# Attention and a long convolution on one core: VectorE's exponential passes in halves, new planning clocks, half a q projection moved forward

## The chip, the cores and the metric

The kernel runs on one core of a Trainium2 chip. The metric is device time in microseconds of a run. The core's engines are TensorE (PE in the profile; PEld is its weight load), VectorE (DVE), ScalarE (ACT), GpSimd (POOL) and SyncE (SP, which here issues most DMAs). Each takes its instructions in the order in which they were written for it, and they wait for one another by semaphores.

## The reference

Two independent computations over 2048 positions and 512 channels, whose results are put side by side. All inputs are bf16.

```python
# A: attention, 32 heads of 16 channels
q, k, v = split(x @ wqkv)
scores = einsum("bhqd,bhkd->bhqk", q, k) * 16 ** -0.5
a = einsum("bhqk,bhkd->bhqd", softmax(scores), v)  ->  merged heads @ wo

# B: a short shift convolution, then a convolution as long as the sequence
kv = (sum over t of k_pad[:, t:t+2048, :] * shift_k[:, 3-t]) * v
y = irfft(rfft(kv, 4096) * rfft(ssm_k, 4096))[:2048] + kv * ssm_D
b = q * y
out = concatenate([a, b], axis=-1)
```

The scores have 32 x 2048 x 2048 elements, and each of them needs an exponential.

## The kernel before

**Blocks and chunks.** Attention is cut into 2048 blocks of 128 keys by 512 queries of one head. A block of scores is one matmul into one bank of the matmul accumulator PS (line L678 in `emit_qk`), and a chunk `T` is three blocks, at the start and the end two: 695 chunks. Chunks use banks 0 to 2 and 3 to 5 in turn. ScalarE takes the exponential of a chunk in one instruction (L685), from PS into the tile PT. The products with v (`emit_pv`, L773) are matmuls that add up in another bank; a column of ones beside v gives the sums by which the result is divided (`finish_group`, L797 to L814).

**Blocks on VectorE.** For some chunks the third block is left out of ScalarE's instruction, and VectorE makes its exponential. Scores are scaled so that they count in units of 1/65536 of a power of two. A first operation, the fix (L701, in `exp_on_dve`), clamps the block, adds the exponent's offset and writes whole numbers into the tile EI: the upper half of such a number is the exponent, the lower half the fraction. When a set of two or four blocks is full, `passes` records five operations for it (L725, L727, L728, L729 and L731), which work out a polynomial of the fraction in fp16 tiles, and a last one (L735, two blocks at a time) that puts it into the number. Its upper 16 bits, read as bf16, are the exponential, and L773 reads them straight from EI. Each operation waits for the one before it.

**Other work.** TensorE also makes the projections to q, k and v (L395, L402, L436), the short convolution (L460), the long one as matmuls over shifted weights, which are streamed by 512 DMAs into the ring WR (L926), the output projection (L850), and fillers that add zeros (L1071). VectorE copies the results out of PS.

**What sets the order.** The program is planned while it is built. Each engine has a planning clock (`Eng.t`); each recorded operation advances it by a cost in microseconds, and its result counts as seen a little later (`seen_after`). `dve_choice` decides from these clocks whether a chunk gives a block to VectorE: not when VectorE's clock is over `FIX_BEHIND` ahead of TensorE's, not in the last `LAST` chunks, in sets of four from chunk `FULL_AT` on. The passes go into the list `dve_fill`, and are written between VectorE's other operations where they fit ahead of the next fix, as `FIX_LATE` and `NEXT` allow, or when a block falls due. TensorE's queue is filled likewise: `emit_bg` puts projections and convolution between scores and products as far as the clock says that there is time. Ahead of the loop over chunks, the first projection of q and 128 keys are made; the second projection of q is made behind the first chunk's scores, in `bg_step` at `T == 0`.

Of the kernel before, what the change touches and what calls it, by code (L numbers as in the profile page):

```python
# [6 lines left out]
ALU = mybir.AluOpType  # L7
# [28 lines left out]
R_PT = 5  # L36
# [14 lines left out]
OCT = 2.0 ** 16  # L51
ROOT0, ROOT1 = 0.0127173909, 0.9900476185
C0, C1 = 0.3043078141, 0.0780240431
FS = 128.0
BITS = 2.0 ** 23
QSCALE = SCALE * math.log2(math.e) * OCT
FIX_LO = -118.0 * OCT
FIX_ADD = 127.0 * OCT
FULL_AT = 110
UNIT = 1  # L60
OPK = 2
PRODK = 2
TIME = 0.7
FULL = 4
APART = 1
OPEN_STEPS = 4
ROOM = {2: 4.0, 4: 8.0}
LATE = 9.0
CLOSE = 6.0
LAST = 12  # L70
PAIRS_AT_END = 22
SPLIT = 2
FIX_BEHIND = 1.2
NEXT = -0.2
PV_HOLD = 3
LAG_US = 0.068
SPAN = 3.4
SHARE = 0.9
SLACK = 0.06
FIX_LATE = 0.7  # L80
FILL_LATE = 0.5
HARD = 0.7
OPE = 1
FETCH = 256
FETCH_AT = 192
# [25 lines left out]
class Eng:  # L111
# [24 lines left out]
    def op(self, fn, deps=(), inc=True, us=None, late=FILL_LATE, fill=False, counted=False):  # L136
        waits = []
        ready = max([0.0] + [self.at[(id(d[0]), d[1])] for d in deps if d])
        while self.fill and not fill and self.t + self.fill[0][0] <= ready + late:
            self.fill.pop(0)[1]()  # L140
        for d in deps:
            if d is None:
                continue
            sm, v = d
            self.t = max(self.t, self.at[(id(sm), v)])
            if self.seen.get(id(sm), 0) < v:
                self.seen[id(sm)] = v
                waits.append((sm, v))
        if counted:
            c = Count()  # L150
            fn(c)
            n = c.n + max(len(waits) - 1, 0)
            late, self.fetch = self.stall(n, us)
            self.t += late
            self.count += n
        self.t += self.us if us is None else us
        self.last = [x for x in self.last if x[0] > self.t - SPAN] + [(self.t, self.us if us is None else us)]
        if inc:
            self.n += 1
            self.at[(id(self.sem), self.n)] = self.t + self.seen_after  # L160
        self.ops.append((waits, fn, self.sem if inc else None))
        return (self.sem, self.n)
# [21 lines left out]
def bass_concat_heads__mha_block__ssm_conv_h3__prompt_kernel(  # L184
# [24 lines left out]
    def sb(name, shape, dt=BF16):  # L209
# [47 lines left out]

    at = {}
    pe, act, dve, pool, sp = [Eng(sem(n), at, us, after) for n, us, after in (
        ("s_pe", 0.5, 0.11), ("s_act", 0.5, 0.16), ("s_dve", 0.69, 0.06), ("s_pool", 0.5, 0.1), ("s_sp", 0.05, 0.1))]  # L260

    queue = [0.0]

# [150 lines left out]
    def evac_unit(u, bank, h, eng=None):  # L414
        kind = u[0]
        if kind == "q":
            _, qb, g = u
            assert qb != 1 or all((c, 2 + g // 4) in h_prod for c in range(4))
            hh = dve.op(lambda e: e.tensor_scalar(QT[:, qb % 2, g, :], PS[:, bank, :], QSCALE, None, ALU.mult),  # L419
                        [h])  # L420
            h_q[(qb, g)] = hh
        else:
            _, o, sc = u
            dst = KTo[:, o, sc * 512:(sc + 1) * 512]
            if eng is act:
                hh = act.op(lambda e: e.activation(dst, PS[:, bank, :], ACT.Copy), [h])
            else:
                hh = dve.op(lambda e: e.tensor_copy(dst, PS[:, bank, :]), [h])  # L428
            h_k[(o, sc)] = hh
        bank_free[bank] = hh  # L430
# [20 lines left out]
    def unit(u, bank, eng=None):  # L451
        evac_unit(u, bank, pe_unit(u, bank), eng)
# [88 lines left out]
    h = k_part(0, 128)  # L541
    h_k0 = act.op(lambda e: e.activation(KTo[:, 0, 0:128], PS[:, 7, 0:128], ACT.Copy), [h])
    bank_free[7] = h_k0
    evac_unit(("q", 0, 0), 6, hq)


    NBLK = NQB * NG * KT * 4
    size, plan, b_ = [], {}, 0
    while b_ < NBLK:
        T = len(size)  # L550
        n = min(2 if (T % 2 == 1 and T < N_EARLY) or NBLK - b_ <= TAIL else 3, NBLK - b_)
# [106 lines left out]
    h_blk = {}  # L658
    h_ptfree, pt_used = {}, {}
# [9 lines left out]
    def emit_qk(T):  # L669
        bl, banks = chunks[T]  # L670
        deps = qk_deps(T)
        assert None not in deps or T < 8

        def fn(e):
            ins = None
            for b, bank in zip(bl, banks):
                qb, g, kt, s = blk(b)
                ins = e.matmul(PS[:, bank, :],  # L678
                               lhsT=KTo[32 * s:32 * s + 32, g // 2, kt * 128:(kt + 1) * 128],
                               rhs=QT[32 * s:32 * s + 32, qb % 2, g, :],  # L680
                               start=True, stop=True, tile_position=(32 * s, 0))
            return ins
        h = pe.op(fn, deps, us=0.32)
        n = len(bl) - (bl[-1] in on_dve)
        h_exp[T] = act.op(lambda e: e.activation(PT[:, T % R_PT, 0:n * QB],  # L685
                                                 PS[:, banks[0]:banks[0] + n, :].rearrange("p b f -> p (b f)"),
                                                 ACT.Exp, scale=math.log(2.0) / OCT),
                          [h] + h_ptfree.get(T - R_PT, []), us=0.427 * n + 0.047)
        assert T < R_PT or pt_used[T - R_PT] == sum(b not in on_dve for b in chunks[T - R_PT][0])
        for b, bank in zip(bl[:n], banks):  # L690
            bank_free[bank] = h_blk[b] = h_exp[T]
        if n < len(bl):
            bank_free[banks[n]] = exp_on_dve(bl[n], banks[n], h, T)

    h_set = [None]
# [12 lines left out]
    def passes(s):  # L708
        ei = EI[:, s.off:s.off + s.k, :]
        frac = ei.bitcast(UINT16).rearrange("p i (f e) -> p i f e", e=2)[:, :, :, 0]  # L710
        ea, eb = EA[:, 0:s.k, :], EX[:, 0:s.k, :] if s.cap == 4 else EA[:, 2:2 + s.k, :]
        old = [st0["x0"]] if s.cap == 4 and all(o.cap == 2 for o in sets if o is not s) else []
        eg = ea.bitcast(BF16)

        now_g = blk_group(rest[0])
        due = len(chunks) + min((len(rest_of[now_g]) + 2) // 3 if blk_group(x) <= now_g else 22 for x in s.blks) + 1
        st = {"h": None}

        def step(rate, fn, *deps):
            us = 0.155 + 0.533 * s.k / rate  # L720

            def run():
                st["h"] = dve.op(fn, [st["h"] or h_set[0]] + list(deps), us=us, fill=True)
            dve_fill.append((us, run, due))
        step(2, lambda e: e.tensor_scalar(eb, frac, FS / OCT, -FS * ROOT0, ALU.mult, ALU.add),  # L725
             *s.fix, *old)
        step(4, lambda e: e.tensor_scalar(ea, eb, FS * (ROOT0 - ROOT1), None, ALU.add))  # L727
        step(2, lambda e: e.tensor_tensor(ea, ea, eb, ALU.mult))  # L728
        step(4, lambda e: e.tensor_scalar(eb, eb, C1 * BITS / FS ** 3, (C0 + C1 * ROOT0) * BITS / FS ** 2,  # L729
                                                 ALU.mult, ALU.add))  # L730
        step(2, lambda e: e.tensor_tensor(eg, ea, eb, ALU.mult))  # L731

        def last(i0, i1, us):
            def run():
                h_set[0] = dve.op(lambda e: e.scalar_tensor_tensor(ei[:, i0:i1, :], ei[:, i0:i1, :], BITS / OCT, eg[:, i0:i1, :],  # L735
                                                                   ALU.mult, ALU.add), [st["h"], h_set[0]], us=us, fill=True)
                for x in s.blks[i0:i1]:
                    h_blk[x] = h_set[0]
            dve_fill.append((us, run, due))
        for i0 in range(0, s.k, SPLIT):  # L740
            last(i0, min(i0 + SPLIT, s.k), 0.155 + 0.533 * min(SPLIT, s.k - i0))

    dve_fill = dve.fill

# [338 lines left out]
    def bg_step(T, lim):  # L1083
        if T >= 150 and not st["wop"] and len(h_v) == 2 * KT and len(h_k) == 16:
            st["wop"] = True
            load_wop(pe_last())
        for item in list(later):
            if item[0] <= T:
                later.remove(item)
                item[1]()  # L1090
        if T == 0:
            unit(("q", 0, 1), 5)
            h = k_part(128, 512)
            bank_free[7] = h_k[(0, 0)] = dve.op(lambda e: e.tensor_copy(KTo[:, 0, 128:512], PS[:, 7, 128:512]), [h])
            return
        if h_kzall[0]:
            load_wr(T)
            if not h_qn:
                load_qn(0, [h_kzp[15]])
        st["time"] = min(st["time"] + (0.78 if T >= CONV_AT else 0.4 if T >= N_EARLY else 0.45), 1.1)  # L1100
        rest = NB * C // 4 - NB * st["qd"] - st["lag"]
        if T >= N_EARLY:
            st["lags"] = min(st["lags"] + rest / max(CONV_END - T, 1.0), 3.0 * LAGS)
        if run_jobs(T, lim):
            run_conv(T, lim)
# [107 lines left out]
    for T in range(NT + 3):  # L1213
# [7 lines left out]
        for b in [b for batch in pvs for b in batch]:  # L1221
            n = blk_group(b)
# [32 lines left out]
    for t in range(4):  # L1255
        wait_busy(when_of(h_otn[(NQB * NG - 1, 2 * (t // 2) + 2)]), 0)
        h = op_mm(qb, t, 7, 8, banks[t])
# [55 lines left out]
```

## Time and profile before

| | |
|---|---|
| median of three runs | 846.3 us (845.18 to 847.07) |
| the profiled execution, its own time | 846.82 us |
| its span in the trace | 845.0 us |
| busy: PE, DVE, ACT, POOL | 85%, 82%, 98%, 7% |
| granted TensorE clock, mean | 0.997 |

Busy is the time in which an engine has at least one instruction under way, so that overlapping instructions count once, while the mean duration of a group counts each in full. Line numbers such as L685 are lines of the kernel before. A bracket behind a row of the timeline says how long the engine had been idle and what ended that.

### The profile page before, as it was taken

What the parts mean: (1) busy time and instruction counts of PE and PEld (TensorE: products, weight loads), DVE (VectorE), ACT (ScalarE), POOL (GpSimd) and SP (SyncE); (2) the same over time, 40 slices, a digit from 0 to 9 for tenths busy, and PEclk for the clock granted to TensorE, in tenths of its full rate; (3) what the DMA queues carried; (4) which work ended last, traced back from release to release, by engine and by line L of the source; (5) the groups of instructions that cost most, each with busy time, mean ns of one, the idle gap of its engine ahead of it and who ended that gap; (6) DMA issues with size and microseconds to landing.
All of it is one profiled execution on the core that took longest, in us unless ns stands there. A gap on an engine that the chain in (4) does not pass through costs nothing.

```text
span 845.0 us, 30581 instructions
## 1 busy us (share of the span) xinstructions
PE 720.2 (85%) x13944; PEld 311.9 (37%) x13944; DVE 696.8 (82%) x937; ACT 829.2 (98%) x701; POOL 62.8 (7%) x68
## 2 busy tenths in 40 slices
PE   8888889888888889888888888888888888988887
PEld 3332333333333332334344433233444444334422
DVE  4226888879999899898999899889899888888884
ACT  6999999999999999999999999999999999999996
POOL 3893000000000001000000000000000000100000
PEclk9999999999999999999999999999999999999999
DMA  9989302059768662487666869237688899646820
GB/s 247 302 313 250 96 1 74 2 139 254 235 187 262 188 212 73 156 250 222 214 217 221 285 214 279 78 106 268 198 256 266 288 294 312 211 157 219 293 54 26
DMA packets 123970, 167.36 MB, mean 198 GB/s; under 512 B 50496, under 2 KB 55616, under 8 KB 123584
## 3 DMA queue, kind: packets, MB, share of 16 engines
q1 hardware_dynamic: 120864, 162.77, 62.1%
q8 instruction: 110, 1.80, 0.8%
q10 hardware_dynamic: 2400, 1.05, 0.6%
q0 software_dynamic: 576, 1.57, 0.5%
q14 instruction: 20, 0.16, 0.1%
HBM read 143.14 MB, written 16.52 MB: 189 GB/s over the span
## 4 chain that ended last, share of the span: by engine, by line
ACT 94%; PE 3%; DMA 1%; DVE 1%; SPq 0%; issue 0%; ACTq 0%
ACT PT L685 93%; DMA WR<-kz_scratch 1%; PE PS L678 1%; PE PS L526 0%; PE PS L436 0%; PE PS L773 0%; SPq L269 0%; PE PS L850 0%; PE PS L926 0%; DVE VAF L447 0%; PE PS L395 0%; PE PS L402 0%; DVE QT L419 0%; ACT QT L866 0%; PE PS L374 0%
## 5 line engine op out<-in xcount | busy, mean ns | idle before, releaser
L685 ACT ACTIVATE PT<-PS 128x1536 bf16<-128x1536 f32 (+1 forms) x695 | 825.2, 1585 | 3.3 <-PE PS L678 3.1
L678 PE MATMUL PS<-QT,KTo 32*128 32x512 bf16 x2048 | 272.1, 385 | 106.7 <-ACT PT L685 91.5
L773 PE MATMUL PS<-PT,VAF 128*32 128x512 bf16 x1828 | 225.7, 390 | 1.1 <-DVE VAF L447 0.7
L926 PE MATMUL PS<-WR,KV 128*22 128x64 bf16 (+15 forms) x8192 | 180.8, 214 | 3.4 <-DMA WR<-kz_scratch 3.0
L701 DVE TENSOR_SCALAR EI<-PS 128x512 int32<-128x512 f32 x220 | 150.2, 688 | 38.9 <-PE PS L678 38.1
L678 PEld LDWEIGHTS PS<-QT,KTo 32*128 32x128 bf16 x2048 | 67.8, 91 | 270.1 <-ACT PT L685 255.6
L926 PEld LDWEIGHTS PS<-WR,KV 128*22 128x22 bf16 (+15 forms) x8192 | 148.6, 120 | 48.4 <-issue 22.5
L735 DVE SCALAR_TENSOR_TENSOR EI<-EI,EA 128x1024 int32<-128x1024 int32 x110 | 134.1, 1219 | 2.1
L773 PEld LDWEIGHTS PS<-PT,VAF 128*32 128x32 bf16 x1828 | 53.9, 93 | 97.9 <-issue 91.9
L725 DVE TENSOR_SCALAR xT<-EI 128x2048 f16<-128x2048 uint16 x48 | 58.7, 1223 | 1.3
L728 DVE TENSOR_TENSOR EA<-EA,xT 128x2048 f16<-128x2048 f16 x48 | 58.4, 1217 | 0.5
L731 DVE TENSOR_TENSOR EA<-EA,xT 128x2048 bf16<-128x2048 f16 x48 | 58.3, 1215 | 0.5
L269 POOL DMA_DIRECT2D out_dram<-OUTA x12 | 7.9, 660 | 661.4 <-DVE OUTA L857 460.6
L1071 PE MATMUL PS<-IDN,ZR 128*32 128x512 bf16 (+3 forms) x664 | 52.4, 330 | 0.0
L773 PE MATMUL PS<-EI,VAF 128*32 128x512 bf16 x220 | 45.3, 410 | 0.0
L395 PE MATMUL PS<-xT,WQP 128*128 128x512 bf16 x128 | 40.3, 385 | 3.3 <-DVE KTo L428 1.7
L850 PE MATMUL PS<-WKV,OTN 128*128 128x512 bf16 x128 | 37.2, 384 | 1.3 <-DVE OUTA L857 0.7
L727 DVE TENSOR_SCALAR EA<-xT 128x2048 f16<-128x2048 f16 x48 | 33.1, 691 | 1.3
L729 DVE TENSOR_SCALAR xT<-xT 128x2048 f16<-128x2048 f16 x48 | 32.9, 686 | 0.5
L797 DVE STREAM_TRANSPOSE DT<-PS 128x512 f32<-128x512 f32 x30 | 21.4, 713 | 11.4 <-PE PS L773 11.4
L419 DVE TENSOR_SCALAR QT<-PS 128x512 bf16<-128x512 f32 x32 | 21.8, 682 | 8.8 <-PE PS L395 8.8
L447 DVE CAST VAF<-PS 128x512 bf16<-128x512 f32 (+1 forms) x17 | 11.2, 656 | 17.1 <-PE PS L436 17.0
(74 smaller groups left out, 367.1 us busy)
## 6 DMA issues: line engine op xcount, KB each, us to landing
WR<-kz_scratch SPq DMA_DIRECT2D x512, 256.0 KB
kz_scratch<-WR SPq DMA_DIRECT2D x16, 752.0 KB, 5.8
QN<-in_B_q_dram SPq DMA_DIRECT2D x16, 128.0 KB, 4.0
out_dram<-KV SPq DMA_DIRECT2D x16, 128.0 KB, 4.5
out_dram<-OUTA POOLq DMA_DIRECT2D x12, 128.0 KB, 2.2
QT<-in_B_ssm_k_dram SPq DMA_DIRECT2D x1, 1024.0 KB, 5.5
EI<-in_B_ssm_k_dram SPq DMA_DIRECT2D x1, 1024.0 KB, 8.9
OTN<-in_B_v_dram SPq DMA_DIRECT2D x1, 1024.0 KB, 5.9
```

Source lines behind the costliest of these rows:

```text
L395: return e.matmul(PS[:, bank, :], lhsT=WQP[:, dc, g, :], rhs=xT[:, dc, qb * 512:(qb + 1) * 512], start=(dc == 0), stop=(dc == 3))
L678: ins = e.matmul(PS[:, bank, :], lhsT=KTo[32 * s:32 * s + 32, g // 2, kt * 128:(kt + 1) * 128], rhs=QT[32 * s:32 * s + 32, qb % 2, g, :], ...
L685: h_exp[T] = act.op(lambda e: e.activation(PT[:, T % R_PT, 0:n * QB], PS[:, banks[0]:banks[0] + n, :].rearrange("p b f -> p (b f)"), ACT.E ...
L701: s.fix.append(dve.op(lambda e: e.tensor_scalar(EI[:, i, :], PS[:, bank, :], FIX_LO, FIX_ADD, ALU.max, ALU.add), [h] + old + [x for o in s ...
L725: step(2, lambda e: e.tensor_scalar(eb, frac, FS / OCT, -FS * ROOT0, ALU.mult, ALU.add), *s.fix, *old)
L728: step(2, lambda e: e.tensor_tensor(ea, ea, eb, ALU.mult))
L731: step(2, lambda e: e.tensor_tensor(eg, ea, eb, ALU.mult))
L735: h_set[0] = dve.op(lambda e: e.scalar_tensor_tensor(ei[:, i0:i1, :], ei[:, i0:i1, :], BITS / OCT, eg[:, i0:i1, :], ALU.mult, ALU.add), [s ...
L773: ins = e.matmul(PS[32 * s:32 * s + 32, pvb(qb * NG + g), :], lhsT=VAF[:, kt, h * VW:h * VW + 32], rhs=rhs, start=(order[b] == 0), stop=(o ...
L850: ins = e.matmul(PS[:, bank, :], lhsT=OTN[:, oslot(qb * NG + g), t * 128:(t + 1) * 128], rhs=WOP[:, g, :], start=(g == 0), stop=(g == NG - 1))
L926: ins = e.matmul(PS[32 * c:32 * c + NW - 2 * n, BGB, col:col + 64], lhsT=KV[:, 2 * n:NW, 4 * qd + c], rhs=w, start=(n == 0), stop=(n == NB ...
L1071: ins = e.matmul(PS[32 * c:32 * c + 32, pvb(n), 0:128 * k], lhsT=ZR[:, :], rhs=IDN[:, :].rearrange("p (m d) -> p m d", m=1).broadcast_to([ ...
```

## The change

- **Passes in halves.** `passes` now cuts a set into two halves (of two blocks, or of one in a set of two). Each of the six operations is recorded for the first half and then for the second, and each waits for the operation before it on its own half, not for the other half's. The last operation's results count as done by halves.
- **Planning clocks.** VectorE's operations are planned 0.084 us shorter, and their results are seen 0.12 us later instead of 0.06. An exponential of n blocks is planned at 0.41 n + 0.1 instead of 0.427 n + 0.047.
- **Thresholds and weights of the planner**, among them those shown below.
- **Half a q projection.** Two of the four matmuls of the second q projection stand ahead of the loop over chunks, the other two where all four stood.

```diff
-FULL_AT = 110
+FULL_AT = 90
-TIME = 0.7
+TIME = 0.8
-CLOSE = 6.0
-LAST = 12
+CLOSE = 4.0
+LAST = 10
-SPLIT = 2
-FIX_BEHIND = 1.2
-NEXT = -0.2
+DVE_OVER = 0.084
+DVE_SEEN = 0.12
+FIX_BEHIND = 1.6
+NEXT = -0.1
-FIX_LATE = 0.7
+FIX_LATE = 0.4
+Q1 = 2
...
-        self.t += self.us if us is None else us
+        self.t += (self.us if us is None else us) - (DVE_OVER if self.us == 0.69 else 0.0)
...
-        ("s_pe", 0.5, 0.11), ("s_act", 0.5, 0.16), ("s_dve", 0.69, 0.06), ("s_pool", 0.5, 0.1), ("s_sp", 0.05, 0.1))]
+        ("s_pe", 0.5, 0.11), ("s_act", 0.5, 0.16), ("s_dve", 0.69, DVE_SEEN), ("s_pool", 0.5, 0.1), ("s_sp", 0.05, 0.1))]
...
     evac_unit(("q", 0, 0), 6, hq)
+    pe_unit(("q", 0, 1), 5, range(Q1))
...
-                          [h] + h_ptfree.get(T - R_PT, []), us=0.427 * n + 0.047)
+                          [h] + h_ptfree.get(T - R_PT, []), us=0.41 * n + 0.1)
...
-        st = {"h": None}
-
-        def step(rate, fn, *deps):
-            us = 0.155 + 0.533 * s.k / rate
+        st, width = {}, (s.k + 1) // 2
+        def piece(rate, make, deps, i0, i1, ends):
+            us = 0.155 + 0.533 * (i1 - i0) / rate
 
             def run():
-                st["h"] = dve.op(fn, [st["h"] or h_set[0]] + list(deps), us=us, fill=True)
-            dve_fill.append((us, run, due))
+                h = dve.op(make(slice(i0, i1)), [st.get(i0, h_set[0])] + deps, us=us, fill=True)
+                st[i0] = h
+                if ends:
+                    h_set[0] = h
+                    for x in s.blks[i0:i1]:
+                        h_blk[x] = h
+            return us, run, due
+
+        def step(rate, make, deps=(), ends=False):
+            for i0 in range(0, s.k, width):
+                dve_fill.append(piece(rate, make, list(deps), i0, min(i0 + width, s.k), ends))
...
-            unit(("q", 0, 1), 5)
+            evac_unit(("q", 0, 1), 5, pe_unit(("q", 0, 1), 5, range(Q1, 4)))
```

Counted over the whole order, VectorE gets 244 fixes instead of 220; ScalarE's 695 exponentials are 414 of three blocks and 281 of two, instead of 438 and 257; the sets are 52 of four blocks and 18 of two, instead of 48 and 14, and their passes 840 instructions instead of 420; the fillers on TensorE fall from 664 matmuls to 564. The lines of the changed kernel are numbered two to nine higher: the fix is L704, the passes L737 to L744, the exponential L688, the scores L681, the q projection L397.

TensorE, at the start: warm-up, turning x, the first q projection (into PS from WQP), 128 keys, the first chunk's scores. Before:

```order
L395 MATMUL PS<-xT,WQP 128x512 x4
L538 MATMUL PS<-xT,WKV 128x128 x4
L678 MATMUL PS<-QT,KTo 128x512 x3
L395 MATMUL PS<-xT,WQP 128x512 x4
L538 MATMUL PS<-xT,WKV 128x384 x4
L678 MATMUL PS<-QT,KTo 128x512 x2
```

And now:

```order
L397 MATMUL PS<-xT,WQP 128x512 x4
L540 MATMUL PS<-xT,WKV 128x128 x4
L397 MATMUL PS<-xT,WQP 128x512 x2
L681 MATMUL PS<-QT,KTo 128x512 x3
L397 MATMUL PS<-xT,WQP 128x512 x2
L540 MATMUL PS<-xT,WKV 128x384 x4
L681 MATMUL PS<-QT,KTo 128x512 x2
```

Two of the second projection's matmuls moved from behind the first scores to ahead of them.

VectorE, in the middle of the run: the passes of a set of four (EI, EA and xT are the sets' tiles) with fixes (EI from PS) and copies between them. Before:

```order
L731 TENSOR_TENSOR EA<-EA,xT 128x2048
L735 SCALAR_TENSOR_TENSOR EI<-EI,EA 128x1024 x2
L725 TENSOR_SCALAR xT<-EI 128x4x512
L727 TENSOR_SCALAR EA<-xT 128x2048
L728 TENSOR_TENSOR EA<-EA,xT 128x2048
L701 TENSOR_SCALAR EI<-PS 128x512
L729 TENSOR_SCALAR xT<-xT 128x4x512
L701 TENSOR_SCALAR EI<-PS 128x512 x3
```

And now:

```order
L743 TENSOR_TENSOR EA<-EA,xT 128x1024 x2
L744 SCALAR_TENSOR_TENSOR EI<-EI,EA 128x1024 x2
L861 CAST OUTA<-PS 128x512
L737 TENSOR_SCALAR xT<-EI 128x2x512 x2
L739 TENSOR_SCALAR EA<-xT 128x1024 x2
L740 TENSOR_TENSOR EA<-EA,xT 128x1024 x2
L741 TENSOR_SCALAR xT<-xT 128x2x512
L704 TENSOR_SCALAR EI<-PS 128x512
L741 TENSOR_SCALAR xT<-xT 128x2x512
L704 TENSOR_SCALAR EI<-PS 128x512
```

Each pass is now two instructions of half the size, one for each half, and a fix may stand between the two.

ScalarE, in the first third: exponentials of three blocks (1536 columns) and of two (1024), in runs. Before:

```order
L685 ACTIVATE PT<-PS 128x1536 x8
L685 ACTIVATE PT<-PS 128x1024 x4
L685 ACTIVATE PT<-PS 128x1536 x6
L685 ACTIVATE PT<-PS 128x1024 x4
L685 ACTIVATE PT<-PS 128x1536 x8
L685 ACTIVATE PT<-PS 128x1024 x4
```

And now:

```order
L688 ACTIVATE PT<-PS 128x1536 x6
L688 ACTIVATE PT<-PS 128x1024 x4
L688 ACTIVATE PT<-PS 128x1536 x5
L688 ACTIVATE PT<-PS 128x1024 x4
L688 ACTIVATE PT<-PS 128x1536 x6
L688 ACTIVATE PT<-PS 128x1024 x4
```

Each run of four short ones is a set of four on VectorE; fewer long ones stand between two such sets.

More of the change, by code (lines that the diff above doesn't have):

```diff
@@ L725, in passes @@
[L725 to L741, printed above, removed]
+                h = dve.op(make(slice(i0, i1)), [st.get(i0, h_set[0])] + deps, us=us, fill=True)
@@ new lines, in run @@
+                st[i0] = h
[7 more added lines that the diff above has]
+                dve_fill.append(piece(rate, make, list(deps), i0, min(i0 + width, s.k), ends))
+        step(2, lambda sl: lambda e: e.tensor_scalar(eb[:, sl], frac[:, sl], FS / OCT, -FS * ROOT0, ALU.mult, ALU.add),
+             s.fix + old)
@@ new lines, in passes @@
+        step(4, lambda sl: lambda e: e.tensor_scalar(ea[:, sl], eb[:, sl], FS * (ROOT0 - ROOT1), None, ALU.add))
+        step(2, lambda sl: lambda e: e.tensor_tensor(ea[:, sl], ea[:, sl], eb[:, sl], ALU.mult))
+        step(4, lambda sl: lambda e: e.tensor_scalar(eb[:, sl], eb[:, sl], C1 * BITS / FS ** 3,
+                                                     (C0 + C1 * ROOT0) * BITS / FS ** 2, ALU.mult, ALU.add))
+        step(2, lambda sl: lambda e: e.tensor_tensor(eg[:, sl], ea[:, sl], eb[:, sl], ALU.mult))
@@ L743, in bass_concat_heads__mha_block__ssm_conv_h3__prompt_kernel @@
+        step(1, lambda sl: lambda e: e.scalar_tensor_tensor(ei[:, sl], ei[:, sl], BITS / OCT, eg[:, sl], ALU.mult, ALU.add),
+             ends=True)
     dve_fill = dve.fill
```

## The prediction

> **What bounds the kernel now.** I read the page first: busy time of each engine, the chain that ended last, the largest group.
>
> ```profile
> PE 720.2 (85%) x13944; PEld 311.9 (37%) x13944; DVE 696.8 (82%) x937; ACT 829.2 (98%) x701; POOL 62.8 (7%) x68
> ACT PT L685 93%; DMA WR<-kz_scratch 1%; PE PS L678 1%; PE PS L526 0%; PE PS L436 0%; PE PS L773 0%; SPq L269 0%; PE PS L850 0%; PE PS L926 0%; DVE VAF L447 0%; PE PS L395 0%; PE PS L402 0%; DVE QT L419 0%; ACT QT L866 0%; PE PS L374 0%
> L685 ACT ACTIVATE PT<-PS 128x1536 bf16<-128x1536 f32 (+1 forms) x695 | 825.2, 1585 | 3.3 <-PE PS L678 3.1
> ```
>
> ScalarE's exponentials are the kernel: 695 of them fill 825.2 us of a span of 845.0 and are 93% of the chain, with 3.3 us of idle before them in all. Whatever shortens this row shortens the kernel, as long as nothing else begins to hold it up. The mean of 1585 ns is no price, though: 695 times it is 1102 us, so neighbours overlap. The price is the step from one start to the next, read from ScalarE's timeline with a window that is opened further and further:
>
> ```profile
> 400.62 2.72 ACT L685 ACTIVATE PT<-PS 128x1536 bf16<-128x1536 f32 x2
> 400.62 4.06 ACT L685 ACTIVATE PT<-PS 128x1536 bf16<-128x1536 f32 x3
> 400.62 4.98 ACT L685 ACTIVATE PT<-PS 128x1536 bf16<-128x1536 f32 x4
> ```
>
> One more exponential adds 1.34 us or 0.92 us: three blocks of scores, or two. Check: the order has 438 of three and 257 of two before, and 438 x 1.34 + 257 x 0.92 = 823 us, against 825.2 in the row. **A block of scores that VectorE takes is worth 0.42 us of ScalarE.**
>
> The second question is who serves VectorE and who waits for it: the table of waits, then a stretch of the windows without start and end.
>
> ```profile
> DVE EI L701 <- PE PS L678: 38.1, 91, 2.5
> ACT PT L685 <- PE PS L678: 3.1, 5, 1.0
> PE PS L678 <- DVE EI L701: 1.4, 5, 0.4
> 110.00:830.00 720.00, 614.08 (x13102) 273.04 (x13099) 637.92 (x834) 718.40 (x603) 7.92 (x12) 1.00 0.63 196
> ```
>
> VectorE (the third figure with a count, 637.92) is idle 82 us of these 720, and its first operation on a block (L701, the "fix") waited 38.1 us for scores in the whole run: VectorE is early. The scores (L678) waited for a fix five times, 1.4 us in all. So VectorE has room, and TensorE's clock is at 1.00.
>
> **The change part by part.** *More blocks on VectorE.* The order has 244 fixes instead of 220, and exponentials of 414 and 281 instead of 438 and 257. ScalarE loses 24 x 0.42 = **10.1 us**, all of it on the path. That is the main term; the new costs and thresholds of the planner count only through it and through where things stand.
>
> *The passes in halves.* VectorE's timeline shows what a pass costs behind one that it needs, and behind one that it doesn't:
>
> ```profile
> 512.63 1.22 DVE L731 TENSOR_TENSOR EA<-EA,xT 128x2048 bf16<-128x2048 f16 x1
> 513.88 2.49 DVE L735 SCALAR_TENSOR_TENSOR EI<-EI,EA 128x1024 int32<-128x1024 int32 x2
> 516.40 1.23 DVE L725 TENSOR_SCALAR xT<-EI 128x2048 f16<-128x2048 uint16 x1
> 517.66 0.70 DVE L727 TENSOR_SCALAR EA<-xT 128x2048 f16<-128x2048 f16 x1
> 518.39 1.23 DVE L728 TENSOR_TENSOR EA<-EA,xT 128x2048 f16<-128x2048 f16 x1
> 519.53 0.69 DVE L701 TENSOR_SCALAR EI<-PS 128x512 int32<-128x512 f32 x1
> 520.13 0.68 DVE L729 TENSOR_SCALAR xT<-xT 128x2048 f16<-128x2048 f16 x1
> 520.73 1.45 DVE L701 TENSOR_SCALAR EI<-PS 128x512 int32<-128x512 f32 x2
> ```
>
> L725 to L727 is 1.26 us for an operation of 1.23: a dependent pass starts 0.03 to 0.04 after the end. But L728 to the fix is 1.14 for 1.23, the fix to L729 0.60 for 0.69, and L729 to the next fix 0.60 for 0.68: an independent operation starts about 0.085 **before** the end. A chain of whole passes on a set of four blocks therefore costs 1.26 + 0.73 + 1.26 + 0.73 + 1.25 + 2.52 = 7.75 us. Halves taken in turn are independent neighbours, at the durations of these forms:
>
> ```profile
> L701 DVE TENSOR_SCALAR EI<-PS 128x512 int32<-128x512 f32 x220 | 150.2, 688 | 38.9 <-PE PS L678 38.1
> L735 DVE SCALAR_TENSOR_TENSOR EI<-EI,EA 128x1024 int32<-128x1024 int32 x110 | 134.1, 1219 | 2.1
> L939 DVE CAST YB<-PS 128x256 bf16<-128x256 f32 x23 | 9.7, 421 | 6.8 <-PE PS L926 6.0 <-PE PS L1071 0.4 <-PE PS L773 0.4
> L725 DVE TENSOR_SCALAR EA<-EI 128x1024 f16<-128x1024 uint16 x14 | 9.7, 690 | 0.4
> L727 DVE TENSOR_SCALAR EA<-EA 128x1024 f16<-128x1024 f16 x14 | 5.9, 425 | 0.4
> L939 DVE CAST YB<-PS 128x128 bf16<-128x128 f32 x4 | 1.1, 286 | 1.0 <-PE PS L926 1.0
> ```
>
> A half of two blocks is three passes like L725's, two like L727's and the last one: 3 x 0.690 + 2 x 0.425 + 1.219 = 4.14 us of durations, less 6 x 0.085, so 3.63; there are 104, 377 us. A half of one block has no row; its nearest are 0.421 (as many steps as 512 at double rate), 0.286 and, for the last pass, 0.688: 3 x 0.421 + 2 x 0.286 + 0.688 - 0.51 = 2.01, an estimate; there are 36, 73 us. Before: 48 x 7.75 = 372, and 14 sets of two at 4.14 + 6 x 0.04 = 4.38, 61 us. So 450 us against 433: twice the instructions for 24 blocks more cost VectorE only 17 us. The new fixes add 24 x 0.60 = 14.5. Together +31.5 us, against 82 of idle: VectorE is left some 50 us, none on the path. A half also keeps a fix behind it waiting 0.6 us rather than 1.2. If this cover goes, the second rival is the price.
>
> *Planning clocks.* They issue nothing; they move fixes, the products that use them (L773) and fillers. Before, the planner gave a fix 0.69 us where the trace steps by 0.60, so real time was ahead of the plan; now the plan has no such reserve. A fix that comes late holds the scores two chunks on (same bank), and TensorE's queue behind them. Bounds: nothing, and, where one fix in ten is late by the mean of the old waits (1.4/5 = 0.28 us), 24 x 0.28 = 6.7 us. I take as much again as the old waits, now uncovered: +1.4, since only five of 220 fixes held anything up.
>
> *Half a q projection ahead.* The start, from the timeline of all engines:
>
> ```profile
> 8.26 0.69 DVE L419 TENSOR_SCALAR QT<-PS 128x512 bf16<-128x512 f32 x1 [1.21 <-PE PS L395]
> 9.01 0.39 PE L678 MATMUL PS<-QT,KTo 32*128 32x512 bf16 x3 [0.56 <-DVE QT L419]
> 9.33 1.04 PE L395 MATMUL PS<-xT,WQP 128*128 128x512 bf16 x4
> 9.44 1.45 ACT L685 ACTIVATE PT<-PS 128x1536 bf16<-128x1536 f32 x1 [0.69 <-PE PS L678]
> 11.15 0.39 PE L678 MATMUL PS<-QT,KTo 32*128 32x512 bf16 x2
> 11.58 2.37 ACT L685 ACTIVATE PT<-PS 128x1024 bf16<-128x1024 f32 x2 [0.69 <-PE PS L678]
> ```
>
> TensorE waits 0.56 us for VectorE's copy of the first q; two of the four matmuls (1.04 us, so some 0.5) now lie there, and the first scores hardly move (0 to 0.1 us). Behind them only two are left, so the second scores come some 0.4 us earlier, out of ScalarE's gap of 0.69. ScalarE could start on them from 9.44 + 1.34 = 10.78, so all of that counts. I take **-0.4**, and between -0.45 and +0.1.
>
> *Nothing at the end.* The stalls that are left lie late, where the convolution's weights arrive late:
>
> ```profile
> 788.61 0.26 PE L926 MATMUL PS<-WR,KV 128*32 128x64 bf16 x4 [1.83 <-DMA WR<-kz_scratch]
> 789.24 17.97 ACT L685 ACTIVATE PT<-PS 128x1536 bf16<-128x1536 f32 x15 [0.97 <-PE PS L678]
> 807.79 4.63 ACT L685 ACTIVATE PT<-PS 128x1024 bf16<-128x1024 f32 x4 [0.58 <-PE PS L678]
> ```
>
> ScalarE loses 0.97 + 0.58 = 1.55 us to them. The weights (512 loads on SP's queue) are the same, needed at a pace 1% higher; the plan may meet these two arrivals or others: -1.55 to about +2 us, taken at 0.
>
> **The sum.** Span 845.0 - 10.1 - 0.4 + 1.4 = 835.9 us. That execution took 846.82 us, 1.82 outside the span: 837.7. It stood 0.5 above the median of the runs, 846.3: **837.2 us**.
>
> **The rivals.**
>
> *The reserve was needed.* The same sum with the upper bound of late fixes, or a bit more where weights add theirs: 846.3 - 10.1 - 0.4 + 6.7 to 9 = 842.5 to 844.8 or, where the fixes give back all of it, 845 to 847. For it: VectorE goes from 82 us of idle to 50 and its waits for scores must shrink; against it: five short waits in 220.
>
> *Halves that don't overlap: slower.* Place: each of 840 passes on VectorE. All evidence for 0.085 us is from pairs with a fix or another operation on PSUM on one side. If a half in fast mode lets the next start only at its end, the passes cost 104 x 4.14 + 36 x 2.52 = 521 us, 88 more than before, and with fixes at 0.688 it is +105 us. Of that 82 is room, 23 is not: 846.3 + 23 = 869 us, and 888 if half of the 38 us of waits stays. It decides from the point where the room left over (82 - 31.5 - 10 of a shorter ScalarE = 40 us over 840 halves, 48 ns each) is used up, that is where the overlap is under 37 ns. Against it, two copies between SBUF tiles that need nothing of each other:
>
> ```profile
> 16.77 0.62 DVE L359 COPY WQP<-OTN 128x256 bf16<-128x256 bf16 x4
> ```
>
> Four in 0.62 us, steps far under any fixed part: the overlap is there without PSUM, too. A rule speaks for this rival: the Trainium skill, "VectorE: DVE Perf Modes", sections "The DRAIN you can't avoid" and "Rules for kernel authors", has it that the next VectorE operation starts only when the pipeline of the last has emptied, semaphores or not, and that one should lower the number of operations. By that rule this change would be the 869 us above. This trace disagrees with it as far as independent neighbours go (0.60 us steps for 0.69).
>
> *The change does little*: the order shows the 24 blocks moved, so that the count is not in doubt; this is no case of its own.
>
> **How the numbers follow.** Forecast (834 to 841): 0.72. Reserve needed: 0.14 for 841 to 844.6, 0.05 for a full loss within 0.2% of 846.3 (1.7 us, about what a measurement of this kernel can tell from no change). Halves without overlap, or VectorE as the bound in some other way: 0.09. So faster 0.86, same 0.05, slower 0.09. The range: at its low end no late fix and no late weights, 846.3 - 10.1 - 0.4 - 1.55 = 834.2; at its high end most of the second case, 843.5.
>
> **What would show it.** Right: exponentials of about 815 us with idle of 2 to 5 us before them; steps of about 0.60 us between alternating halves of 0.69, and 0.34 between those of 0.425; VectorE idle some 50 us in the middle; the second exponential near 11.1 us; scores waiting for a fix under 4 us in all. Wrong: halves stepping by 0.69 or more, VectorE without a gap, and ScalarE waiting for scores that wait for L704 (the fix's new line); or late weights of several us.

## The result, and the profile after

The changed kernel takes 842.46 us (median of 20 runs, 839.08 to 850.16) against 847.93 us for the kernel before (20 runs, 845.18 to 852.88). The ratio is 0.9944 with a 95% interval of 0.9928 to 0.9960: faster by 4.7 us, where the forecast was 0.9892, or 9.1 us. The sign is right, and the gain is half of what was forecast. The ratio and its interval are worked out from the single runs, so that the ratio differs a little from that of the two medians (0.9935).

The profiled execution took 842.29 us with a span of 840.5. Busy time, the largest group, the waits that matter, and the stretch from 110 to 830 us (VectorE is the third figure with a count):

```profile
PE 710.0 (84%) x13793; PEld 313.6 (37%) x13844; DVE 750.4 (89%) x1379; ACT 820.9 (98%) x701; POOL 62.0 (7%) x68
L688 ACT ACTIVATE PT<-PS 128x1536 bf16<-128x1536 f32 (+1 forms) x695 | 816.9, 1456 | 6.1 <-PE PS L681 5.3
DVE EI L704 <- PE PS L681: 8.6, 18, 2.6
PE PS L681 <- DVE EI L704: 5.3, 16, 0.9
PE PS L930 <- issue: 4.1, 6, 1.2
ACT PT L688 <- PE PS L681: 5.3, 15, 0.7
110.00:830.00 720.00, 608.08 (x12983) 275.36 (x13021) 689.61 (x1244) 715.15 (x608) 7.15 (x12) 0.99 0.63 196
```

The exponentials went from 825.2 to 816.9 us, 8.3 less and not 10.1, and the idle ahead of them from 3.3 to 6.1. VectorE now hardly waits for scores (8.6 us, before 38.1), and scores wait for its fixes (5.3 us, before 1.4). New is "issue": TensorE stops with nothing to wait for that the profile shows, 4.1 us ahead of the convolution alone. In the span, 4.5 us shorter, one part is no effect of the change: the first exponential starts at 10.61 us, 9.44 in the profile before. The twelve warm-up matmuls took 5.30 us here and 4.20 there; they step by 0.43 us until TensorE's clock rises, and it rose later here. This differs from one execution to the next: later profiles of two kernels that share the old start had 10.35 and 10.49 us, and one with the new start (whole passes, below) had 9.48.

The row of all ScalarE instructions in order of time breaks where ScalarE had to wait. These twelve breaks follow the start:

```profile
179.98 1.02 ACT L688 ACTIVATE PT<-PS 128x1024 bf16<-128x1024 f32 x1 [0.34 <-PE PS L681]
181.49 164.41 ACT L688 ACTIVATE PT<-PS 128x1536 bf16<-128x1536 f32 x139 [0.48 <-PE PS L681]
346.07 11.06 ACT L688 ACTIVATE PT<-PS 128x1024 bf16<-128x1024 f32 x10 [0.18 <-PE PS L681]
357.62 1.02 ACT L688 ACTIVATE PT<-PS 128x1024 bf16<-128x1024 f32 x1 [0.49 <-PE PS L681]
358.82 258.28 ACT L688 ACTIVATE PT<-PS 128x1024 bf16<-128x1024 f32 x219 [0.18 <-PE PS L681]
617.57 1.02 ACT L688 ACTIVATE PT<-PS 128x1024 bf16<-128x1024 f32 x1 [0.46 <-PE PS L681]
618.85 1.02 ACT L688 ACTIVATE PT<-PS 128x1024 bf16<-128x1024 f32 x1 [0.25 <-PE PS L681]
620.31 93.44 ACT L688 ACTIVATE PT<-PS 128x1024 bf16<-128x1024 f32 x79 [0.44 <-PE PS L681]
714.22 61.34 ACT L688 ACTIVATE PT<-PS 128x1024 bf16<-128x1024 f32 x52 [0.47 <-PE PS L681]
775.86 1.02 ACT L688 ACTIVATE PT<-PS 128x1024 bf16<-128x1024 f32 x1 [0.30 <-PE PS L681]
777.06 20.81 ACT L688 ACTIVATE PT<-PS 128x1024 bf16<-128x1024 f32 x17 [0.18 <-PE PS L681]
798.25 34.70 ACT L688 ACTIVATE PT<-PS 128x1024 bf16<-128x1024 f32 x31 [0.38 <-PE PS L681]
```

An exponential of two blocks alone takes 1.02 us where the step in a run is 0.92: each break costs some 0.1 us beside its idle time. There are three kinds. The one near 355 us begins on VectorE; its timeline and TensorE's:

```profile
351.24 0.39 PE L681 MATMUL PS<-QT,KTo 32*128 32x512 bf16 x3
351.76 0.76 DVE L739 TENSOR_SCALAR EA<-xT 128x1024 f16<-128x1024 f16 x2
352.44 0.68 DVE L740 TENSOR_TENSOR EA<-EA,xT 128x1024 f16<-128x1024 f16 x1
353.04 0.68 DVE L704 TENSOR_SCALAR EI<-PS 128x512 int32<-128x512 f32 x1
353.64 0.70 DVE L801 STREAM_TRANSPOSE DT<-PS 128x512 f32<-128x512 f32 x1
353.87 0.39 PE L681 MATMUL PS<-QT,KTo 32*128 32x512 bf16 x3 [0.89 <-DVE EI L704]
355.45 0.61 PE L681 MATMUL PS<-QT,KTo 32*128 32x512 bf16 x3
355.99 1.04 PE L777 MATMUL PS<-PT,VAF 128*32 128x512 bf16 x7
```

The scores of 351.24 were there at 351.63, but three halves of passes went first and their fix started at 353.04, 1.4 us late. The scores two chunks on waited for it at 353.87, TensorE was idle for 0.89 us, the group's old sums (L801) came late too, and then scores take 0.61 us instead of 0.39: TensorE runs at half its clock for 3.4 us.

The second kind has no VectorE in it:

```profile
615.23 0.28 PE L930 MATMUL PS<-WR,KV 128*18 128x64 bf16 x8
616.71 0.49 PE L930 MATMUL PS<-WR,KV 128*14 128x64 bf16 x28 [1.21 <-issue]
711.86 0.39 PE L777 MATMUL PS<-PT,VAF 128*32 128x512 bf16 x2
713.11 0.39 PE L777 MATMUL PS<-PT,VAF 128*32 128x512 bf16 x2 [0.86 <-issue]
```

TensorE stops in the middle of a batch that was recorded as one piece. Counted in the program (two instructions for a matmul, its weight load and the multiplication, and one for each further wait), the four such stops of over 0.5 us stand ahead of the 193rd or 194th instruction of a block of 256. The table of DMA queues shows what moves in such blocks:

```profile
q8 instruction: 109, 1.79, 0.9%
```

The trace holds these 109 packets one by one. Each has 16,384 bytes, and there is one for every 256 of TensorE's 27,994 instructions; from this they are taken to be its own. Paired in order with the boundaries, they explain the stops: in all four TensorE went on 1.20 to 1.43 us after the end of the packet, and at no other boundary did it go on sooner than 1.20 us after it. So the instructions arrived late. The kernel's planner knows these boundaries (`FETCH_AT = 192`, `FETCH = 256`) and holds weight loads back around them, by its clocks. The kernel before had 0.3 us of such idle ahead of its convolution.

The third kind, near 180 us, begins with neither:

```profile
177.00 0.45 PE L681 MATMUL PS<-QT,KTo 32*128 32x512 bf16 x3 [0.95 <-ACT PT L688]
179.32 0.61 PE L681 MATMUL PS<-QT,KTo 32*128 32x512 bf16 x3
```

TensorE waited 0.95 us for ScalarE, as it may, since it was ahead; then its clock fell to half from 177.2 to 180.6 us, and the next scores came late. Of the 4.15 us of idle in the twelve breaks, 2.00 stand behind the second kind (617.57 to 714.22, and 798.25), 1.33 behind late work on VectorE (346.07 to 358.82, and 775.86 and 777.06, a few us behind the fourth stop, at 770.20) and 0.82 behind the third kind.

### The profile page after: what moved, and what is told of

Same layout as the page of the kernel before. It is cut to its first block, busy times and chain, and to the rows that moved or that the text cites. A ratio compares the mean times of both kernels' runs of the same rounds, so it can differ in the third digit from the quotient of the medians.

```text
span 840.5 us, 30799 instructions
## 1 busy us (share of the span) xinstructions
PE 710.0 (84%) x13793; PEld 313.6 (37%) x13844; DVE 750.4 (89%) x1379; ACT 820.9 (98%) x701; POOL 62.0 (7%) x68
## 4 chain that ended last, share of the span: by engine, by line
ACT 86%; PE 7%; DVE 5%; issue 1%; DMA 1%; SPq 0%; ACTq 0%; DVEq 0%
ACT PT L688 86%; PE PS L681 2%; PE PS L777 2%; DVE xT L737 1%; PE PS L854 1%; DVE EI L704 1%; PE PS L930 1%; PE PS L528 1%; DMA WR<-kz_scratch 1%; DVE QT L421 0%; PE PS L397 0%; DVE EI L744 0%; DVE EA L740 0%; DVE OUTA L861 0%; DVE EA L739 0%
## 5 line engine op out<-in xcount | busy, mean ns | idle before, releaser
L688 ACT ACTIVATE PT<-PS 128x1536 bf16<-128x1536 f32 (+1 forms) x695 | 816.9, 1456 | 6.1 <-PE PS L681 5.3
L681 PE MATMUL PS<-QT,KTo 32*128 32x512 bf16 x2048 | 274.6, 387 | 106.0 <-ACT PT L688 83.2
L930 PE MATMUL PS<-WR,KV 128*4 128x64 bf16 (+15 forms) x8192 | 181.0, 214 | 4.8 <-issue 4.1
L704 DVE TENSOR_SCALAR EI<-PS 128x512 int32<-128x512 f32 x244 | 163.6, 685 | 9.1 <-PE PS L681 8.6
L930 PEld LDWEIGHTS PS<-WR,KV 128*32 128x32 bf16 (+15 forms) x8192 | 148.0, 120 | 48.8 <-issue 26.8
L681 PEld LDWEIGHTS PS<-QT,KTo 32*128 32x128 bf16 x2048 | 69.2, 91 | 258.9 <-ACT PT L688 233.8
L744 DVE SCALAR_TENSOR_TENSOR EI<-EI,EA 128x1024 int32<-128x1024 int32 (+1 forms) x140 | 147.0, 1080 | 0.0
L737 DVE TENSOR_SCALAR xT<-EI 128x1024 f16<-128x1024 uint16 x104 | 67.4, 688 | 1.9
L743 DVE TENSOR_TENSOR EA<-EA,xT 128x1024 bf16<-128x1024 f16 x104 | 68.8, 682 | 0.0
L740 DVE TENSOR_TENSOR EA<-EA,xT 128x1024 f16<-128x1024 f16 x104 | 68.3, 683 | 0.0
L741 DVE TENSOR_SCALAR xT<-xT 128x1024 f16<-128x1024 f16 x104 | 41.0, 419 | 0.0
L739 DVE TENSOR_SCALAR EA<-xT 128x1024 f16<-128x1024 f16 x104 | 39.8, 419 | 0.0
L397 PE MATMUL PS<-xT,WQP 128*128 128x512 bf16 x103 | 33.8, 387 | 4.5 <-issue 1.4
L801 DVE STREAM_TRANSPOSE DT<-PS 128x512 f32<-128x512 f32 x30 | 21.4, 713 | 4.0 <-PE PS L777 3.7
```

The lines of the kernel that those rows point to most:

```text
L681: ins = e.matmul(PS[:, bank, :], lhsT=KTo[32 * s:32 * s + 32, g // 2, kt * 128:(kt + 1) * 128], rhs=QT[32 * s:32 * s + 32, qb % 2, g, :], ...
L704: s.fix.append(dve.op(lambda e: e.tensor_scalar(EI[:, i, :], PS[:, bank, :], FIX_LO, FIX_ADD, ALU.max, ALU.add), [h] + old + [x for o in s ...
L737: step(2, lambda sl: lambda e: e.tensor_scalar(eb[:, sl], frac[:, sl], FS / OCT, -FS * ROOT0, ALU.mult, ALU.add), s.fix + old)
L740: step(2, lambda sl: lambda e: e.tensor_tensor(ea[:, sl], ea[:, sl], eb[:, sl], ALU.mult))
L741: step(4, lambda sl: lambda e: e.tensor_scalar(eb[:, sl], eb[:, sl], C1 * BITS / FS ** 3, (C0 + C1 * ROOT0) * BITS / FS ** 2, ALU.mult, AL ...
L743: step(2, lambda sl: lambda e: e.tensor_tensor(eg[:, sl], ea[:, sl], eb[:, sl], ALU.mult))
```

## The experiments

Theories: (A) VectorE has become late: its reserve is used up, and fixes and copies come late. (B) TensorE's instructions come late behind the convolution's weight loads. (C) The half-clock windows come from too few fillers. (D) A block is worth less than 0.42 us.

**VectorE lighter, order kept.** In `passes`:

```diff
-        ei = EI[:, s.off:s.off + s.k, :]
+        w = slice(0, 256)
+        ei = EI[:, s.off:s.off + s.k, w]
...
-        ea, eb = EA[:, 0:s.k, :], EX[:, 0:s.k, :] if s.cap == 4 else EA[:, 2:2 + s.k, :]
+        ea, eb = EA[:, 0:s.k, w], EX[:, 0:s.k, w] if s.cap == 4 else EA[:, 2:2 + s.k, w]
```

> The changed kernel with the same order, but each of VectorE's passes covers 256 of a block's 512 columns (the other columns of those blocks keep the fix's whole numbers, so this part of the result is left out). VectorE loses some 160 us of work. Theory, VectorE has become late: the scores' waits for fixes (5.3 us in the changed kernel) fall under 1 us, TensorE's half-clock windows in the middle go from four to none or one, ScalarE's idle falls to 3 us or less, and the time is 0.988 to 0.990 of the kernel before (836.5 to 838.5 us). Rival, the loss comes from TensorE alone (too few fillers, stops while it fetches instructions): windows and stops stay, and the time stays at 0.9944.

Measured: 0.9894 (0.9865 to 0.9923). The breaks near 180 and 357 us are gone, and the waits of scores for fixes fall to 0.5 us. The profile still has these rows:

```profile
L688 ACT ACTIVATE PT<-PS 128x1536 bf16<-128x1536 f32 (+1 forms) x695 | 815.8, 1508 | 5.2 <-PE PS L681 4.6
PE PS L681 <- DVE EI L704: 0.5, 1, 0.5
PE PS L931 <- DMA WR<-kz_scratch: 3.3, 3, 1.4
PE PS L931 <- issue: 3.0, 4, 1.4
```

The time is as A forecast, 4.2 us below the changed kernel (interval about 2.8 to each side), but idle did not fall to 3 us, and three half-clock windows are left in the middle, not one or none. A holds for the first kind of break. The break near 180 us is gone too, but A does not explain that: TensorE waits the same 0.95 us for ScalarE here, at 176.66 us, only its clock stays up. Stops and late weights, all behind 615 us, are another matter.

**Small weight loads, order kept.** In `load_wr`:

```diff
+            n = LROW if qd < 4 else 256
...
-                          ap=[[NB * VG, 128 // VG], [LKZ, VG], [1, LROW]])
+                          ap=[[NB * VG, 128 // VG], [LKZ, VG], [1, n]])
-            h_wr[qd] = dma(sp, d_wr[r], WR[r][:, c, :], src,
+            h_wr[qd] = dma(sp, d_wr[r], WR[r][:, c, 0:n], src,
```

> The changed kernel with the same order, but from the fifth quad on each load of convolution weights brings a quarter of the bytes (the convolution uses stale weights in the rest, so its result is left out). Theory, TensorE's stops of about 1 us in which it waits for nothing that the profile shows (4.1 us ahead of the convolution in the changed kernel) come from its instructions arriving late behind these loads: the stops go, the half-clock window near 616 us goes with them, and the time falls by 1.5 to 2.5 us to about 0.992. Rival, VectorE's lateness is all of it: stops or not, the time stays within 0.5 us of the changed kernel, 0.9944.

Measured: 0.9881 (0.9860 to 0.9903), 5.3 us better than the changed kernel (about 2.3 to each side) and so more than B gave. ScalarE's row has no break behind 358 us, and TensorE no stop of over 0.5 us:

```profile
L688 ACT ACTIVATE PT<-PS 128x1536 bf16<-128x1536 f32 (+1 forms) x695 | 815.8, 1501 | 3.5 <-PE PS L681 2.7
PE PS L931 <- issue: 0.5, 1, 0.5
PE PS L681 <- DVE EI L704: 3.8, 12, 0.9
```

The rival (VectorE's lateness is all of it) falls. The instruction packets show the link: behind 300 us they ended, in the median, 3.7 us ahead of the instructions at the boundary, and 2.8 us with full loads in the same order. They took as long (0.99 and 0.98 us), so they started later. Where they wait, at the DMA engines or ahead of them, no run here shows.

**The same edit on the kernel before, as a control.**

> The kernel before with loads of a quarter of the bytes from the fifth quad on (the convolution's result is left out), a control for the same edit on the changed kernel. If the stops that these loads cause are a loss that the change added, before loses little without them: its two waits for weights cost ScalarE 1.55 us, so 0.997 to 0.999 of the time before. If the loads cost every plan as much, it is 0.993 to 0.994, as much as the changed kernel gained by the same edit.

Measured: 0.9973 (0.9959 to 0.9987), 2.3 us, within the first case. Loads cost the kernel before 2.3 us and the changed one 5.3: the change added 3.0 us of this, with some 2.6 us of uncertainty to each side.

**Both edits together.**

> The changed kernel in its own order with both edits, VectorE's passes on 256 of 512 columns and small weight loads (both parts' results left out). If late work on VectorE and stops behind loads are all that the 24 blocks' gain was lost to, no idle over 0.3 us is left between exponentials and the time is 0.985 to 0.988 of the kernel before, that is the 10.1 + 0.4 us that were forecast and before's own 1.5 of waits for weights. Rival, the blocks are worth less than 0.42 us each: ScalarE has no idle and the time is still above 0.989.

Measured: 0.9855 (0.9829 to 0.9881). Its row and that of the control, one below the other:

```profile
L688 ACT ACTIVATE PT<-PS 128x1536 bf16<-128x1536 f32 (+1 forms) x695 | 814.9, 1543 | 1.7 <-PE PS L681 1.3
```

```profile
L685 ACT ACTIVATE PT<-PS 128x1536 bf16<-128x1536 f32 (+1 forms) x695 | 825.0, 1582 | 2.4 <-PE PS L678 2.3
```

825.0 - 814.9 = 10.1 us for 24 blocks, and 0.9855 / 0.9973 = 0.988, 10 us of 847.5, in the timed runs. Apart from 0.69 us at the start, no idle of over 0.3 us is left. With nothing late, the change brings what was forecast of it; D falls. Against small loads alone (0.9881), lightening VectorE is worth 2.2 us, which by itself is not clear of noise (about 2.9 to each side); with full loads it was worth 4.2. Taken away singly the two losses are 4.2 and 5.3 us, together 7.5, so that their shares depend on which goes first.

**More fillers.** `SHARE = 1.0` instead of 0.9; there are 956 filler matmuls, not the 984 of the expectation.

> The changed kernel with the planner asked to keep TensorE busy for all of each stretch and not 0.9 of it: 984 filler matmuls instead of 564, still 244 blocks on VectorE. Theory, TensorE's half-clock windows come from too few fillers: the four windows go and the time falls by 2 to 3 us, to 0.991. Rival, the windows arise where no filler can stand, at a change of group while VectorE has not yet taken the old sums out of their bank: they stay, and the time is the same or up to 2 us longer for fillers in the way of scores.

Measured: 0.9922 (0.9899 to 0.9944), not told apart from the changed kernel. Two half-clock windows in the middle instead of four, and the idle of ScalarE is 6.1 us as before: other stops take their place, one of 1.90 and one of 1.50 us. C is no more than a part: the four windows went, as it says, and two came up elsewhere.

**Whole passes.** `st, width = {}, s.k`.

> The changed kernel with the passes whole again, and all new clocks and thresholds kept: the planner gives VectorE 236 blocks, 8 fewer than with halves. Theory, the room for more blocks is in good part the halves' doing: ScalarE's work rises by 8 x 0.42 = 3.4 us, the chains of whole passes cost VectorE their gaps again, and the time is 3 to 5 us above the changed kernel, 0.998 to 1.000. Rival, the clocks and thresholds do all of it: the time is that of the changed kernel, 0.993 to 0.995.

Measured: 1.0035 (1.0007 to 1.0063), slower than the kernel before, and worse than either expectation. Scores waited 10.5 us for fixes (30 times), TensorE's stops ahead of the convolution were 6.5 us and its waits for weights 5.5:

```profile
L688 ACT ACTIVATE PT<-PS 128x1536 bf16<-128x1536 f32 (+1 forms) x695 | 821.4, 1397 | 11.6 <-PE PS L681 10.6
PE PS L681 <- DVE EI L704: 10.5, 30, 0.8
```

Of the 7.7 us above the changed kernel 3.4 are the 8 blocks; the rest is idle and broken runs. Without the halves the new clocks and thresholds bring nothing.

**Halves alone.** The kernel before with the new `passes`.

> The kernel before with the passes in halves alone, under its old planning clocks, which charge each half in full: the planner gives VectorE 212 blocks, 8 fewer. Theory, halves save VectorE time that only the new clocks turn into blocks: 8 x 0.42 = 3.4 us more on ScalarE, 1.003 to 1.005. Rival, halves shorten waits on the path by themselves: 0.998 to 1.001.

Measured: 1.0071 (1.0048 to 1.0094). The 8 blocks fewer give 3.4 of 6 us. Scores no longer wait for fixes, but TensorE stops for 3.5 us ahead of the convolution and 2.3 ahead of fillers: another order, other stops. Neither halves nor clocks gain anything by themselves.

**A reserve in VectorE's clock.** `DVE_OVER = 0.065`.

> The changed kernel with a reserve in VectorE's planning clock: operations are planned 0.065 us shorter than their durations, not 0.084, and the planner gives VectorE 234 blocks instead of 244. ScalarE's exponentials grow by 10 x 0.42 = 4.2 us. Theory, the missing reserve lost 2 to 2.5 us of idle on ScalarE: the waits for fixes fall under 3 us, and the time is 1 to 3 us above the changed kernel, 0.995 to 0.998. Rival, the reserve is worth as much as the blocks: 0.993 to 0.995, at a third fewer half-clock windows.

Measured: 0.9997 (0.9980 to 1.0013), above both. Waits for fixes fell to 3.0 us, as A says, but weights were late by 6.7 us, behind which ScalarE lost up to 1.41 us at a time, and it lost 1.44 behind a stop of 1.62. The reserve takes blocks and leaves stops and late weights.

**Attempts at a faster version.** Longer holds for weight loads (`LEAD = 6.0`, `FETCH_GOES = 0.6`):

> The changed kernel with weight loads held back over a longer stretch ahead of each boundary of 256 TensorE instructions (LEAD 6.0 and FETCH_GOES 0.6 instead of 4.0 and 1.2), an attempt at a faster version. If the stops at these boundaries come from loads that land then, they go and the time is 0.990 to 0.992; if the plan's clock is not close enough to real time for such holds, stops or waits for weights stay and it is 0.994 or more.

Measured: 0.9963 (0.9938 to 0.9988). Stops ahead of the convolution fell to 2.4 us, and waits for weights rose from 0.5 to 6.2. Fillers with a small reserve (`SHARE = 1.0`, `DVE_OVER = 0.075`):

> An attempt at a faster version: the changed kernel with fillers for all of each stretch (980 filler matmuls) and 0.075 us in VectorE's planning clock, 242 blocks. If fewer half-clock windows and a small reserve both help: 0.989 to 0.991. If the stops at boundaries behind weight loads rule, as they did with fillers alone: 0.992 to 0.994.

Measured: 0.9939 (0.9920 to 0.9957). One half-clock window in the middle, fixes waited for 3.2 us, and stops of up to 1.62 us are left. Fillers with passes let in less (`SHARE = 1.0`, `FIX_LATE = 0.2`):

> An attempt at a faster version: the changed kernel with fillers for all of each stretch and passes let in ahead of a fix only where they delay it by 0.2 us at most in the plan (0.4 in the changed kernel); 244 blocks still. If passes ahead of fixes cause the waits of scores: waits for fixes 2 to 3 us instead of 5.3, time 0.989 to 0.991; if not, 0.992 to 0.994.

Measured: 0.9946 (0.9925 to 0.9967), waits for fixes 4.8 us, stops of up to 1.87. None is told apart from the changed kernel as a gain.

## Why the prediction was right and wrong

- **The blocks, -10.1 us: right.** 10.1 between the profiles of the control and of both edits together.
- **Half a q projection, -0.4: right in size.** ScalarE's gap ahead of its second exponential was 0.69 us in three profiles with the old start and 0.25 or 0.26 in all with the new one. The time of 11.1 us did not come (12.32), since the start itself was later; a timed run could not show 0.4 us.
- **The halves: right.** The rows at 351.76 and 352.44 above: two of 0.42 us in 0.76, so a step of 0.34, and 0.60 from L740 to the fix behind it. The half of one block has 0.418 to 0.421, 0.284 to 0.288 and 0.683 us, estimated at 0.421, 0.286 and 0.688. Halves without a need of each other overlap by 0.08 us, and the rival of 869 us is out. The rule of the Trainium skill ("VectorE: DVE Perf Modes", "The DRAIN you can't avoid") that the next operation does not start until the pipeline is empty was read too widely in the prediction: the same section adds that a next operation that is not held starts earlier, and the overlap of 0.08 us here is in line with the addition. Whole passes under the same clocks, with half as many operations, were slower.
- **The room on VectorE: mis-sized.** I left 50 us of idle; the profile has 30 (720 - 689.6). The 82 us of idle before held the gaps of 0.03 to 0.04 us behind each dependent pass, some 15 us, and I had charged the same gaps to the passes. The room after was about 35.
- **Late fixes, +1.4: too small.** 2.2 us by the runs with small loads, 4.2 by those with full loads. It was sized by the old waits, though the text said itself that the reserve was gone; the mechanism was named, and the first rival's bound of 6.7 was too much. The time itself, 0.9944 of 846.3 or 841.6 us, lies at the lower edge of that rival's case, but late fixes brought only a part of it there.
- **"Nothing at the end", 0: this is the step that failed.** It looked at two late arrivals of weights in the profile before and took the loads as the same. They are, but the order that they meet is not, and in the new one they make TensorE's instructions late. The runs give +3.0 us in its place, beyond the bound of 2; taken in the other order, behind the lighter VectorE, it is 1.0. Whichever way they are split, this term and the one before come to 5.2 us (7.5 less the 2.3 of the kernel before, some 2.8 to each side) instead of 1.4. Only late weights were in the bounds; stops by late instructions were not, though the planner's constants name them. The new clocks are not what it takes: halves alone, under the old clocks, had 5.8 us of stops. Why the order before is nearly free of them stays open.
- **TensorE's clock at 1.00: held for the old plan alone.** Four windows at half clock came up in the middle of the profile, one before. Two of them pass a late fix or a stop on to several chunks, one makes a break by itself (near 180 us), and one (481 us) cost ScalarE nothing.

The sum by the runs: 10.1 + 0.4 - 3.0 - 2.2 = 5.3 us, against 4.7 measured. It must come out about so, since the two losses are differences between runs that lead from one kernel to the other; what it tests is that the rest of the way, 10 us with nothing late, is the 10.1 + 0.4 of the forecast. The intervals, 1 to 3 us to each side, allow no closer account.

## What to carry to other kernels

An engine that is not the bottleneck can be filled only up to the point where its order is met in real time: count gaps once, as work or as room, and size the waits by what the new plan leaves, not by what the old one had. Where a program is planned, a change of the plan moves everything that it keeps apart, transfers and instruction boundaries too; a control with that traffic made small, on both kernels, shows at once what it costs. Halving a chain of dependent passes and taking the halves in turn gives back the gaps and the overlap, though the instructions double.

## What the runs showed of the hardware

TensorE stopped for 0.5 to 1.9 us where its next instructions came late. All 33 such stops of 0.5 us or more, in ten of the kernels here, stand at the 193rd or 194th instruction of a block of 256, and in 32 of them TensorE went on 1.20 to 1.58 us after the end of the instruction packet (in the other, 0.72). They came in every new order with full loads and not in the profile of the kernel before; with small loads one of 0.50 us is left.

TensorE's clock fell to half for windows of 3.41 us without any idle of over 1 us, in three of four cases. These are the 3.41 us just ahead of the four falls in the changed kernel, and the same stretch ahead of the scores of 176.66 us with the lighter VectorE, where the clock stayed up:

```profile
173.81:177.22 3.41, 2.16 (x15) 0.51 (x15) 3.34 (x10) 3.41 (x4) 0.00 (x0) 1.00 0.77 153
351.30:354.71 3.41, 1.69 (x40) 0.83 (x42) 3.38 (x8) 3.41 (x4) 0.00 (x0) 1.00 0.79 229
477.59:481.00 3.41, 2.14 (x58) 1.04 (x56) 3.29 (x7) 3.41 (x4) 0.00 (x0) 1.00 0.79 253
614.12:617.53 3.41, 2.04 (x74) 1.18 (x70) 3.09 (x7) 2.99 (x3) 0.00 (x0) 1.00 0.88 323
```

```profile
173.25:176.66 3.41, 2.15 (x15) 0.50 (x13) 2.98 (x8) 3.41 (x4) 0.00 (x0) 1.00 0.71 142
```

TensorE's busy time is the first figure with a count, and the granted clock is third from the end. TensorE was busy for 50 to 63% ahead of the falls, and for 84% of the stretch from 110 to 830 us; but 63% did not always bring a fall, and the runs give no limit.

How many such windows a kernel meets varies with the execution. Over the 20 runs of the changed kernel the mean granted clock went from 0.980 to 0.996, and the time with it: the three runs at 0.980 to 0.982 took 848.8 to 850.2 us, the four at 0.994 to 0.996 took 839.1 to 842.6. Whether the windows make these runs longer, or stops make both, was not settled.
